# Two transformer layers on one core: slot order of the last down weights, block 3's stores, and the order of squares in layer 1's projection

## The chip, the cores and the metric

The kernel runs on one core of a Trainium2 chip. The time is the device time of one execution in microseconds (us). The engines have queues of their own and run side by side: TensorE (PE) does matmuls, VectorE (DVE) and ScalarE (ACT) work element by element, GpSimd (POOL) does small vector work and issues DMAs, and SyncE (SP) issues DMAs. Each engine works through its own queue in order, so an instruction that waits holds everything behind it on that engine.

## The reference, cut to what matters

```python
def _A_ref(x, wqkv, wo):          # S = 2048 rows, D = 448, 16 heads of 28
    qkv = (x @ wqkv) ...          # split into q, k, v by head
    scores = einsum("bhqd,bhkd->bhqk", q, k) * (Dh ** -0.5)
    o = einsum("bhqk,bhkd->bhqd", softmax(scores), v)
    return o ... @ wo

def _B_ref(x, w_gate, w_up, w_down):        # F = 1792
    return (sigmoid(x @ w_gate) * (x @ w_up)) @ w_down

x = x + _A_ref(layernorm(x), ...)
x = x + _B_ref(layernorm(x), ...)
x = x + _A_ref(layernorm(x), ...)
x = x + _B_ref(layernorm(x), ...)
```

All of it is in float32. The kernel splits each float32 factor into a high and a low float16 part and sums three products for one.

## The kernel before

**Order.** Two layers follow each other. Each is project (layer norm, q, k and v), attend, out_project and gated (the feed-forward). The 2048 rows are 4 blocks of 512, a block is 4 tiles of 128. The order of instructions on every engine is written out by hand: the order of the Python calls is the order of each queue.

**Fast products.** gated, and in layer 1 also the q/k products of blocks 0, 2 and 3 (qk_sums, L884), use a scheme of seven products of half matrices in place of eight. Its operands are sums and differences of quarter matrices. For rows they are made by half_steps into the tiles xwide and xshort; for the q/k weights add_pair (L748) makes them out of raw weights (tile raws) into wsums, five microseconds of DVE work with ACT beside it. There are three pairs of weight tiles (PAIRS_QK); the seventh weight tile is alone and is multiplied in the usual way (L998). Block 1 takes the usual product (qk, L618).

**The end of gated.** The down product of one block is seven products too, with weights dn, one tile of 784 KB for each. The products of block 3 have nothing to run beside, so they come last, in the order TAIL = (0, 1, 3, 2, 5, 4, 6). Product k adds into PSUM bank 3, 1, 3, 2, 3, 1, 3 for k = 0 to 6, except that k = 6 uses banks 0 and 2 here; finish (L1882) lets DVE add a bank to the rows x. Each of the seven takes 42 matmuls. Three dn tiles are held; used_dn (L1766) gives one back and loads the next on POOL's queue (L1758). A list called between puts the preparation of layer 1 between the products: norms, lifts and transposes of block 2's rows (squared, L333 to L358), store and gather (L391, L399), which turn them round through DRAM, and add_pair(2).

**Slots.** SBUF is managed as 19 equal slots (class Slots, "_s" in names) and 12 quarter slots ("_q"). get takes the first of a queue of free slots, put gives a slot back at its end and put_next at its front. A tile in a slot waits for the last user of the tile that was there. So the order of get and put decides which load waits for whom.

**Layer 1's start.** project for layer 1 runs in this order: q/k of block 0 (qk_sums), its values (vals, L1084, evacuated by ACT at L1102), q/k of block 1 (qk), its values, q/k of block 2 and of block 3 (qk_sums), values of blocks 2 and 3. In qk_sums three Pairs use PSUM banks 0 and 1, 2 and 3, and 6 and 7, each a chain and a side. ACT copies each product off the chain (L956) ahead of the next one there. Then high (ACT, L917) and low (DVE, L921) cut a finished tile into its parts and store it. square (ACT, L932) and two maxima (DVE, L936) bound the norms of heads; small matmuls (norms, L899) sum them into a bank, and finish (L1067) reduces it. The work named in points and after is done between products: it prepares the rows of the blocks to come.

Of the kernel before, what the change touches and what calls it, by code (L numbers as in the profile page):

```python
# [13 lines left out]
F16 = mybir.dt.float16  # L14
# [5 lines left out]
P = 128  # L20
S = 2048
D = 448
# [99 lines left out]
def interleaved_layers(ctx: ExitStack, tc: tile.TileContext, x_in, wqkv, wo, w_gate, w_up,  # L122
# [531 lines left out]
    class WeightsQKV:  # L654
# [65 lines left out]

        def read_pairs(self):
            self.raws = [big.get("raws", [P, 2, 1024]) for _ in range(2)]
            for j, tiles in enumerate(PAIRS_QK):
                v = self.pair(j)
                for z, i in enumerate(tiles):
                    c = slice(i * P, (i + 1) * P)
                    nc.gpsimd.dma_start(v[:, 0:3, z],
                                        wqkv[0:384, c].rearrange("(s p) n -> p s n", p=P))
                    nc.gpsimd.dma_start(v[0:64, 3, z], wqkv[384:448, c])
                nc.gpsimd.memset(v[64:P, 3], 0.0)  # L730

        def pair(self, j):
            return self.raws[j // 2][:, j % 2].rearrange("p (s z n) -> p s z n", s=4, z=2)

        def load(self):
            self.v = big.get("wv", [P, 2, 4, D], F16)
            self.more = more = big.get("wmore", [P, 8 * P + D], F16)
            self.alone = more[:, 0:8 * P].rearrange("p (i k n) -> p i k n", i=2, k=4)
            self.v_tail = more[:, 8 * P:]
            c = slice(ALONE * P, (ALONE + 1) * P)  # L740
            for i in range(2):
                nc.sync.dma_start(self.alone[:, i, 0:3], qk_parts[i, :, 0:3, c])
                r = slice(64 * i, 64 * i + 64)
                nc.sync.dma_start(self.alone[r, 0, 3], qk_parts[i, r, 3, c])
                nc.sync.dma_start(self.v_tail[r], v_parts[r, i, 3])
            nc.sync.dma_start(self.v, v_parts)
            self.sums = []

        def add_pair(self, j):
            v, t = self.pair(j), big.get("wsums", [P, N_SUMS, P], F16)  # L750
            self.sums.append(t)
            m = [int(i > ALONE) for i in PAIRS_QK[j]]
            by = up[:, m[0]:m[0] + 1]
            if m[0] != m[1]:
                for z in range(2):
                    nc.vector.tensor_scalar(v[:, :, z], v[:, :, z], up[:, m[z]:m[z] + 1], None,
                                            op0=ALU.mult)
                by = ones[:, 0:1]
            split_sums(t, v, by)
            if j > 0:  # L760
                big.put(self.raws[j // 2])

# [51 lines left out]
    def project(layer, wq, begun):  # L814
# [68 lines left out]

        def qk_sums(b, blk, points, before=None):  # L884

# [97 lines left out]
            for t in range(2):  # L983
                for q in (0, 2):
                    x = blk.quarter(q, t)
                    for k in range(2):
                        if q + k == 3:
                            terms += [(t, wq.alone[:, 0, 3], x[:, i, 1]) for i in range(2)]
                        else:
                            terms += [(t, wq.alone[:, i, q + k], x[:, j, k])  # L990
                                      for i, j in ((0, 0), (0, 1), (1, 0))]
# [11 lines left out]
            pb.first()  # L1003
            at(0)
            pa.apart()
            pa.second()
# [8 lines left out]
            if before:  # L1015
                before()
            pa.c11_c22()
# [8 lines left out]
            pa.c12()  # L1026
            pb.c12()
            alone = bank(5 - b % 2, "alone")
            pc = Pair(2, 6)
# [24 lines left out]
            pc.tiles[1].high()  # L1054
            pc.tiles[1].low(pc.two)
            pa.tiles[1].square()
            pb.tiles[1].square()
            lone.square()
            pc.tiles[0].square()
            pc.tiles[1].square()  # L1060
            at(5)

            def finish(whole=True):
                pop(len(late) - (0 if whole else 1))
                if whole:
                    for k in range(2):
                        nc.vector.tensor_reduce(peaks[:, k, b:b + 1],  # L1067
                                                pn[0:H, k * P:(k + 1) * P], axis=AX.X,
                                                op=ALU.max)
            return finish  # L1070
# [91 lines left out]
        else:  # L1162
# [16 lines left out]
            fin = qk_sums(3, b3, {}, fin)  # L1179
        if layer > 0:  # L1180
            big.put(*wq.sums)
            evac[0] = 0
# [50 lines left out]
        def last_values(begun=None):  # L1233
# [6 lines left out]
            if layer > 0:  # L1240
                big.put(wq.v, wq.more)

# [485 lines left out]
    class WeightsGated:  # L1728
# [36 lines left out]

        def used_dn(self):  # L1766
            (big.put_next if self.pairs else big.put)(self.dn.popleft())
            if self.products:
                self.load_dn(nc.gpsimd)

    def gated(layer, first, wt, wq):
# [243 lines left out]
        for b, p in seq:  # L2015
# [58 lines left out]
            if b == NB - 1 and not last and p == NP - 2:  # L2074
                wq.read_pairs()

# [153 lines left out]
```

## Time and profile before

| | us |
|---|---|
| median of 3 runs | 1909.7 |
| lowest, highest | 1909.0, 1911.4 |
| the profiled execution, in all | 1910.1 |
| its span, first to last instruction | 1908.4 |

The mean TensorE clock granted over the span is 0.996 of full speed. The page's busy strip for PE and its clock strip:

```profile
PE   9999999999999999999898999999999999999999
...
PEclk9999999999999999999899999999999999999999
```

Each digit is the busy share of a fortieth of the span (47.7 us) in tenths; 9 is 90% or more. Digits 20 to 23, 906 to 1097 us, hold the end of layer 0 and layer 1's projection. In a row of a timeline stand the start, the length, the engine, the line of the kernel, the operation, out<-in, the shape and the count of instructions merged; in square brackets the idle time ahead of it and what ended it. A row of the list of waits reads: engine, what it was to do, what it waited for, then the total in us, how often, and the longest. A row of the window table gives the stretch, its length, the busy time of PE, PE's weight loads, DVE, ACT and POOL with counts, PE's clock, and the DMA engines' share and GB/s.

### The profile page before, as it was taken

What the parts mean: (1) busy time and instruction counts of PE and PEld (TensorE: products, weight loads), DVE (VectorE), ACT (ScalarE), POOL (GpSimd) and SP (SyncE); (2) the same over time, 40 slices, a digit from 0 to 9 for tenths busy, and PEclk for the clock granted to TensorE, in tenths of its full rate; (3) what the DMA queues carried; (4) which work ended last, traced back from release to release, by engine and by line L of the source; (5) the groups of instructions that cost most, each with busy time, mean ns of one, the idle gap of its engine ahead of it and who ended that gap; (6) DMA issues with size and microseconds to landing.
All of it is one profiled execution on the core that took longest, in us unless ns stands there. A gap on an engine that the chain in (4) does not pass through costs nothing. (4 is left out here: it accounts for less than half of the span.)

```text
span 1908.4 us, 57171 instructions
## 1 busy us (share of the span) xinstructions
PE 1884.7 (99%) x24531; PEld 1364.3 (71%) x24531; DVE 1478.9 (77%) x2984; ACT 1425.9 (75%) x1885; POOL 250.5 (13%) x482
## 2 busy tenths in 40 slices
PE   9999999999999999999898999999999999999999
PEld 4456655556566899999776566666666668999999
DVE  7758989898977887778776577877787788877664
ACT  6569999999984655555466799999999746555541
POOL 3023102222102012112310000000000021111110
PEclk9999999999999999999899999999999999999999
DMA  7675444343324745656543411221120246566553
GB/s 250 192 217 160 133 122 131 111 124 117 102 87 131 252 177 206 238 206 244 182 151 105 115 47 31 52 51 33 46 52 12 73 148 231 196 228 225 216 207 140
DMA packets 116472, 273.79 MB, mean 143 GB/s; under 512 B 14478, under 2 KB 72590, under 8 KB 116080
## 3 DMA queue, kind: packets, MB, share of 16 engines
q0 software_dynamic: 33120, 163.33, 23.8%
q1 hardware_dynamic: 81936, 105.33, 19.7%
q8 instruction: 194, 3.18, 0.7%
q10 hardware_dynamic: 1152, 1.38, 0.3%
q14 instruction: 70, 0.57, 0.1%
HBM read 210.98 MB, written 50.62 MB: 137 GB/s over the span
## 5 line engine op out<-in xcount | busy, mean ns | idle before, releaser
L1519 ACT ACTIVATE prob_s<-sc 128x1536 f32<-128x1536 f32 (+1 forms) x657 | 888.7, 1477 | 7.5 <-PE sc L1504 6.8
L1555 PE MATMUL acc<-prob_s,val_s 128*32 128x256 f32 (+3 forms) x7700 | 575.0, 384 | 0.1
L1504 PE MATMUL sc<-qp_s 114*32 114x512 f16 x7868 | 558.1, 379 | 0.7 <-DMA qp_s<-g_scr 0.7
L633 PEld LDWEIGHTS <-gu_s 128*128 128x128 f16 x4368 | 426.7, 98 | 46.1 <-PE op L1684 0.7
L1504 PEld LDWEIGHTS <-qp_s 114*32 114x32 f16 x8192 | 279.8, 96 | 198.3 <-issue 84.9
L1555 PEld LDWEIGHTS acc<-prob_s,val_s 128*32 128x32 f32 x7700 | 282.0, 110 | 130.3 <-issue 12.8
L1864 PE MATMUL dnp<-dn_s,hparts_s 128*128 128x224 f16 x2184 | 248.9, 261 | 8.0 <-DMA dn_s<-dn_parts 8.0
L633 PE MATMUL chain<-xwide_s,gu_s 128*128 128x256 f16 x2016 | 247.5, 273 | 0.1
L1864 PEld LDWEIGHTS <-hparts_s 128*128 128x128 f16 x2184 | 211.9, 99 | 14.4 <-DMA dn_s<-dn_parts 8.2
L1535 DVE SCALAR_TENSOR_TENSOR power_q<-power_q,expo_q 128x512 f32<-128x512 f32 x243 | 168.2, 692 | 8.3
L1937 ACT COPY one_q<-chain 128x256 f32<-128x256 f32 x224 | 82.3, 372 | 113.5 <-PE chain L633 113.0
L1953 DVE TENSOR_TENSOR one_q<-side,one_q 128x512 f32<-128x512 f32 x112 | 72.1, 686 | 96.0 <-PE side L633 95.7
L633 PE MATMUL side<-xshort_s,gu_s 128*128 128x256 f16 x1120 | 140.6, 273 | 0.0
L1745 POOL DMA_DIRECT2D gu_s<-gu_parts x104 | 56.5, 543 | 428.0 <-PE side L633 426.5
L1817 ACT CAST hparts_s<-hsums_q 128x256 f16<-128x256 f32 (+1 forms) x152 | 71.5, 485 | 37.0 <-DVE hsums_q L1829 23.4
L1584 DVE STREAM_TRANSPOSE oturned_q<-acc 128x512 f32<-128x512 f32 x32 | 22.9, 717 | 98.2 <-PE acc L1555 98.1
L1555 PE MATMUL acc<-power_q,val_s 128*32 128x256 f32 (+3 forms) x300 | 94.2, 396 | 0.0
L633 PE MATMUL side<-xwide_s,gu_s 128*128 128x256 f16 x672 | 91.6, 273 | 0.0
L618 PE MATMUL qkp<-xhl_s,wqk_s 128*128 128x512 f16 x385 | 86.5, 379 | 0.9 <-ACT wqk_s L235 0.6
L1964 ACT ACTIVATE one_q<-one_q 128x512 f32<-128x512 f32 x56 | 35.3, 630 | 64.2 <-DVE one_q L1953 64.0
L1529 DVE TENSOR_SCALAR expo_q<-aside,base 128x512 f32<-128x512 f32 x81 | 60.6, 748 | 22.5 <-PE aside L1504 22.3
L1821 DVE TENSOR_TENSOR hparts_s<-hsums_q,hparts_s 128x256 f16<-128x256 f32 (+1 forms) x152 | 72.5, 516 | 5.8 <-ACT hparts_s L1817 5.8
(261 smaller groups left out, 2398.7 us busy)
## 6 DMA issues: line engine op xcount, KB each, us to landing
gu_s<-gu_parts POOLq DMA_DIRECT2D x104, 800.0 KB, 5.9
dn_s<-dn_parts POOLq DMA_DIRECT2D x42, 784.0 KB, 7.2
qp_s<-qk_scr SPq DMA_DIRECT2D x96, 224.0 KB
gu_parts<-pack_s POOLq DMA_DIRECT2D x14, 800.0 KB, 3.8
xt_scr<-xs_s SPq DMA_DIRECT2D x48, 224.0 KB
xraw_s<-xt_scr SPq DMA_DIRECT2D x12, 768.0 KB
qk_scr<-qkhl_q SPq DMA_DIRECT2D x35, 256.0 KB
qp_s<-qk_scr SPq DMA_DIRECT2D x64, 112.0 KB
```

Source lines behind the costliest of these rows:

```text
L618: nc.tensor.matmul(pm, w, x, start=(i == 0), stop=(i == len(terms) - 1))
L633: nc.tensor.matmul(pm, a, x, start=(first and i == 0), stop=(i == len(terms) - 1), skip_group_check=True)
L1504: nc.tensor.matmul(ps[32 * j:32 * j + 32, :], hd.k[:, keys], hd.q[:, qb * W:(qb + 1) * W], start=True, stop=True, tile_position=(0, 32 * j))
L1519: nc.scalar.activation(prob[:, 0:n, :], ps[:, 0:n, :], AF.Exp, scale=exp_scale)
L1529: nc.vector.tensor_scalar(y, ps, base2[:, 0:1], -126.0, op0=ALU.mult, op1=ALU.max)
L1535: nc.vector.scalar_tensor_tensor(p, p, c[k], y, op0=ALU.add, op1=ALU.mult)
L1555: nc.tensor.matmul(acc[qb * VC:(qb + 1) * VC, s], v[:, kc % TB, h, :], probs[c * NB + qb][:, s], start=(kc == 0 and a == 0), stop=(kc == N ...
L1817: nc.scalar.copy(to[:, :, 0], a)
L1821: nc.vector.tensor_tensor(to[:, :, 1], a, to[:, :, 0], op=ALU.subtract)
L1864: nc.tensor.matmul(pm, a[:, x, t], w[:, p, y], start=(begin and n == 0 and (j == 0 or alone)), stop=(n == 2), skip_group_check=True)
L1937: nc.scalar.copy(to, pm)
L1953: nc.vector.tensor_tensor(one[m], side[m], one[m], op=ALU.add)
```

## The change

It edits two places. **In gated of layer 0**, only pairs 0 and 1 of the raw q/k weights are read ahead, into one slot; pair 2 is read later, between the second and the third of the last products. Three more dn tiles are loaded ahead of add_pair(0), so that six of the seven are asked for before the last products begin, and a finished dn slot goes to the front of the queue. The tiles wv and wmore are no longer taken here: the lone weights and the last rows of the values' weights (v_tail) go into unused columns of the wsums tiles (now 32 wide), and they and wv are loaded ahead of the last product. **In layer 1's project**, the norms of block 3 move into block 0's q/k products and its lifts, transposes and store into block 0's values, in place of block 2's half steps, which move into block 1's products. In qk_sums the lone tile is cut ahead of the third pair's first tile, the squares of the first two pairs' second tiles are spread between products, and block 2 leaves three squares (lone and third pair) to block 3, which does them one by one (before(False)) and reduces block 2's norms after its second c12.

```diff
-        def read_pairs(self):
-            self.raws = [big.get("raws", [P, 2, 1024]) for _ in range(2)]
+        def read_pairs(self, js):
+            self.raws = big.get("raws", [P, 2, 1024])
...
         def load(self):
-            self.v = big.get("wv", [P, 2, 4, D], F16)
-            self.more = more = big.get("wmore", [P, 8 * P + D], F16)
...
-            nc.sync.dma_start(self.v, v_parts)
-            self.sums = []
+            self.held, self.sums = [], []
         def add_pair(self, j):
-            v, t = self.pair(j), big.get("wsums", [P, N_SUMS, P], F16)
+            v, t = self.pair(j), big.get("wsums", [P, 32, P], F16)
+            self.held.append(t)
+            self.sums.append(t[:, 0:N_SUMS])
...
+        def load_rest(self):
+            self.alone = [t[:, 28:32] for t in self.held[1:]]
+            self.v_tail = self.held[0][:, N_SUMS:29].rearrange("p k n -> p (k n)")[:, 0:D]
+            c = slice(ALONE * P, (ALONE + 1) * P)
+            for i in range(2):
+                nc.sync.dma_start(self.alone[i][:, 0:3], qk_parts[i, :, 0:3, c])
+                r = slice(64 * i, 64 * i + 64)
+                nc.sync.dma_start(self.alone[0][r, 3], qk_parts[i, r, 3, c])
+                nc.sync.dma_start(self.v_tail[r], v_parts[r, i, 3])
+        def load_values(self):
+            self.v = big.get("wv", [P, 2, 4, D], F16)
+            nc.sync.dma_start(self.v, v_parts)
...
-        def qk_sums(b, blk, points, before=None):
+        def qk_sums(b, blk, points, before=None, defer=False):
...
             pb.first()
             at(0)
+            if before:
+                before(False)
...
             if before:
-                before()
+                before(False)
             pa.c11_c22()
...
             pb.c12()
+            if before:
+                before()
             alone = bank(5 - b % 2, "alone")
...
             pc.c11_c22()
+            pa.tiles[1].square()
             pop()
             some(10)
             lone = Tile(alone, ((ALONE, 0), (ALONE, 1)))
             pc.c21()
+            lone.high()
+            lone.low()
             pc.tiles[0].high()
             pc.tiles[0].low(pc.one)
-            lone.high()
-            lone.low()
-            pop()
             pc.c12()
+            pb.tiles[1].square()
+            squares = deque([lone.square, pc.tiles[0].square, pc.tiles[1].square])
+            if not defer:
+                squares.popleft()()
             pc.tiles[1].high()
             pc.tiles[1].low(pc.two)
-            pa.tiles[1].square()
-            pb.tiles[1].square()
-            lone.square()
-            pc.tiles[0].square()
-            pc.tiles[1].square()
+            while squares and not defer:
+                squares.popleft()()
...
             def finish(whole=True):
+                if not whole:
+                    squares.popleft()()
+                    return
...
-            fin = qk_sums(0, blks[0], {0: ready[0:1], 1: ready[1:2], 2: ready[2:3],
-                                       4: ready[3:4]})
-            vals(0, blks[0], {0: both(*h2[0:2]), 1: both(*h2[2:3], s3[0]),
-                              2: both(fin, h2[3]), 3: both(s3[1], h2[4])})
-            fin = qk(1, b1, [both(s3[2], s3[3], s3[6]), both(s3[4], s3[5], s3[7], s3[8]),
-                             both(s3[9], b3.store), both(h2[5], b3.gather), h2[6], h2[7], h2[8]],
-                     None)
+            fin = qk_sums(0, blks[0], {0: ready[0:1] + s3[0:1], 1: ready[1:2], 2: s3[1:2],
+                                       4: ready[2:3], 5: ready[3:4]})
+            vals(0, blks[0], {0: both(s3[2], s3[3], s3[6]), 1: both(fin, s3[4], s3[7]),
+                              2: both(s3[5], s3[8], s3[9], b3.store),
+                              3: both(h2[0], h2[1], b3.gather)})
+            fin = qk(1, b1, h2[2:9], None)
...
-            fin = qk_sums(2, b2, {0: h3[6:7], 1: h3[7:8], 2: h3[8:9], 4: h3[9:10]})
+            fin = qk_sums(2, b2, {0: h3[6:7], 1: h3[7:8], 2: h3[8:9], 4: h3[9:10]}, None, True)
             fin = qk_sums(3, b3, {}, fin)
...
-        def used_dn(self):
-            (big.put_next if self.pairs else big.put)(self.dn.popleft())
+        def used_dn(self, reuse=False):
+            (big.put_next if self.pairs or reuse else big.put)(self.dn.popleft())
...
-                wq.read_pairs()
+                wq.read_pairs((0, 1))
...
             wq.load()
+            for _ in range(3):
+                wt.load_dn(nc.gpsimd)
             wq.add_pair(0)
             wq.add_pair(1)
...
-            between = deque([turns[0:1], turns[1:2], turns[2:5] + turns[6:8],
-                             turns[5:6] + turns[8:] + [third.store],
-                             [third.gather, lambda: wq.add_pair(2)], []])
+            between = deque([turns[0:1], [lambda: wq.read_pairs((2,))] + turns[1:2],
+                             turns[2:5] + turns[6:8], turns[5:6] + turns[8:] + [third.store],
+                             [third.gather, lambda: wq.add_pair(2)],
+                             [wq.load_rest, wq.load_values]])
...
-            wt.used_dn()
+            wt.used_dn(not last)
```

More of the change, by code (lines that the diff above doesn't have):

```diff
@@ L732, in pair @@
         def pair(self, j):
-            return self.raws[j // 2][:, j % 2].rearrange("p (s z n) -> p s z n", s=4, z=2)
+            return self.raws[:, j % 2].rearrange("p (s z n) -> p s z n", s=4, z=2)
         def load(self):
-            self.v = big.get("wv", [P, 2, 4, D], F16)
-            self.more = more = big.get("wmore", [P, 8 * P + D], F16)
[L738 to L745, printed above, removed]
-            nc.sync.dma_start(self.v, v_parts)
-            self.sums = []
+            self.held, self.sums = [], []
         def add_pair(self, j):
-            v, t = self.pair(j), big.get("wsums", [P, N_SUMS, P], F16)
-            self.sums.append(t)
+            v, t = self.pair(j), big.get("wsums", [P, 32, P], F16)
+            self.held.append(t)
+            self.sums.append(t[:, 0:N_SUMS])
             m = [int(i > ALONE) for i in PAIRS_QK[j]]
@@ L759, in add_pair @@
             split_sums(t, v, by)
-            if j > 0:
-                big.put(self.raws[j // 2])
+            self.to_add -= 1
+            if not self.to_add:
+                big.put(self.raws)
+        def load_rest(self):
[10 more added lines that the diff above has]
+            nc.sync.dma_start(self.v, v_parts)
         def load_usual(self):
@@ L987, in qk_sums @@
                         if q + k == 3:
-                            terms += [(t, wq.alone[:, 0, 3], x[:, i, 1]) for i in range(2)]
+                            terms += [(t, wq.alone[0][:, 3], x[:, i, 1]) for i in range(2)]
                         else:
-                            terms += [(t, wq.alone[:, i, q + k], x[:, j, k])
+                            terms += [(t, wq.alone[i][:, q + k], x[:, j, k])
                                       for i, j in ((0, 0), (0, 1), (1, 0))]
@@ L1240, in last_values @@
             if layer > 0:
-                big.put(wq.v, wq.more)
+                big.put(wq.v, wq.held[0])
         return values, heads, last_values
```

17 lines of the change are left out of this document (8 added, 9 removed).

## The prediction, as it was made before the result was known

> **What bounds the kernel now.** I read the page's busy shares first, then TensorE's list of waits, then the timeline and the window table around each wait.
>
> ```profile
> PE 1884.7 (99%) x24531; PEld 1364.3 (71%) x24531; DVE 1478.9 (77%) x2984; ACT 1425.9 (75%) x1885; POOL 250.5 (13%) x482
> ```
> ```profile
> PE dnp L1864 <- DMA dn_s<-dn_parts: 8.0, 1, 8.0
> PE chain L633 <- ACT one_q L956: 3.3, 1, 3.3
> PE chain L633 <- ACT val_s L1102: 1.6, 1, 1.6
> ...
> PE norms L899 <- DVE sq_q L936: 0.9, 4, 0.3
> PE side L633 <- ACT val_s L1102: 0.7, 1, 0.7
> PE side L633 <- DVE one_q L972: 0.7, 2, 0.4
> ```
>
> TensorE (PE) is busy 99% of the span, so an edit pays only if it removes PE's idle time or makes PE run faster. The idle time is a short list, and all six rows lie in one stretch, 923 to 1060 us: the end of layer 0's feed-forward and layer 1's projection, which is what the diff edits. Their sum, 15.2 us, is not the whole prize: a busy matmul can be a slow one.
>
> ```profile
> 945.10:951.00 5.90, 5.83 (x32) 4.76 (x33) 0.00 (x0) 0.72 (x2) 0.00 (x0) 0.50 0.61 244
> 1014.60:1033.00 18.40, 15.73 (x143) 13.59 (x142) 12.24 (x27) 13.86 (x34) 0.00 (x0) 1.00 0.20 58
> 1038.50:1041.00 2.50, 2.47 (x25) 2.15 (x25) 0.28 (x2) 1.00 (x3) 0.00 (x0) 0.77 0.20 58
> 1041.00:1043.00 2.00, 2.00 (x11) 1.45 (x10) 0.00 (x0) 0.00 (x0) 0.00 (x0) 0.50 0.00 0
> ```
>
> In this window table the number ahead of the last two is PE's granted clock. Behind the 8.0 us wait it is 0.50 for 5.9 us: 2.95 us lost. Behind the 3.3 us wait it is 0.77 over 2.5 us and 0.50 over 2.0 us: 0.23 x 2.5 + 0.5 x 2.0 = 1.6 us lost. In the second row PE idles 1.56 and 0.75 us within 4 us and the clock stays 1.00. So I take gaps up to about 2.3 us as free of a clock loss and one of 3.3 us as not.
>
> **The change, part by part.** Times below are those of the profiled execution before.
>
> *A. The last down weights.*
>
> ```profile
> 923.80 13.39 PE L1864 MATMUL dnp<-dn_s,hparts_s 128*128 128x224 f16 x138
> 945.17 19.14 PE L1864 MATMUL dnp<-dn_s,hparts_s 128*128 128x224 f16 x168 [7.97 <-DMA dn_s<-dn_parts]
> 964.14 1.52 PE L633 MATMUL chain<-xwide_s,wsums_s 128*128 128x256 f16 x12
> ...
> 973.70 0.49 PE L998 MATMUL alone<-xwide_s,wmore_s 128*128 128x256 f16 x3
> ```
> ```profile
> 938.71 0.53 POOL L1758 DMA_DIRECT2D dn_s<-dn_parts  x1 [14.42 <-DVE wsums_s L266]
> ```
> ```profile
> 938.20 0.68 DVE L1882 SCALAR_TENSOR_TENSOR x<-dnp,back,x 128x448 f32<-128x448 f32 x1
> ...
> 956.90 0.87 DVE L756 TENSOR_SCALAR raws_s<-raws_s,up 128x512 f32<-128x512 f32 x2
> ...
> 962.13 1.83 DVE L1882 SCALAR_TENSOR_TENSOR x<-dnp,back,x 128x448 f32<-128x448 f32 x3
> ```
>
> PE stops at 937.2 because the fourth product's weights were asked for at 938.71 only: their slot was that of the raw q/k weights, which DVE's split of pair 1 holds until 938.2. With the diff, only one raw slot is taken, wv and the lone tile take none yet, and three loads stand in POOL's queue before add_pair(0). Counting the slot queue by hand gives the fourth product the slot of the last gate weights, free at 923.7, the fifth that of block 1's transposed rows (xs), and the sixth a down slot free at 925. The 8.0 us wait and the 2.95 us of half clock go.
>
> *What is late next.* The fourth product (k=2) adds into the bank of the first (k=0), and DVE reads that bank with the add at 938.20, behind both splits in its queue. So PE restarts at about 938.9: 1.7 us of idle remain. From there 168 matmuls at full clock (138 took 13.39 us, 97 ns each) take 16.2 us, to 955.1.
>
> The moved read_pairs((2,)) puts four DMAs and a memset into POOL's queue between the two norm_two of block 2:
>
> ```profile
> 911.73 0.78 POOL L727 DMA_DIRECT2D raws_s<-in_A_wqkv_dram  x1
> ...
> 913.83 0.54 POOL L729 DMA_DIRECT2D raws_s<-in_A_wqkv_dram  x1
> 914.36 0.33 POOL L730 MEMSET raws_s<- 64x256 f32 x1
> ...
> 941.88 0.22 POOL L346 TENSOR_SCALAR off<-off 128x2 f32<-128x2 f32 x1
> ...
> 942.80 0.18 POOL L333 TENSOR_SCALAR rs<-mv 128x2 f32<-128x2 f32 x1
> ...
> 944.15 0.23 POOL L346 TENSOR_SCALAR off<-off 128x2 f32<-128x2 f32 x1
> ```
>
> They cost 914.69 - 911.73 = 3.0 us. The first norm_two ends at 942.1, the DMAs at 945.1, the second (1.6 us) at 946.7. ACT's two lifts and DVE's two transposes behind them (0.7 us each, overlapping) end at 948.7, the fifth product's add at 949.3, add_pair(2) (956.90 to 962.13, 5.2 us) at 954.5, and the three adds (1.83 us) at 956.4. Bank 0 is read by the third, and layer 1's first product writes bank 0. PE is there at 955.1 and starts at 956.5: **1.4 us of new idle**. The start moves from 964.14 to 956.5: **-7.6 us** (8.0 + 2.95 - 1.7 - 1.4 = 7.8 by terms; I take the timeline). For the new idle, bounds are 0, if the raws' issues overlap DVE's work, and 4, if the raws land late and the clock halves too; 1.4 is what the rows give.
>
> The fifth load waits for the xs store, and all of POOL's queue behind it: the sixth and seventh loads and norm_two, of which nothing else is due before 940.5.
>
> ```profile
> 926.96 3.55 SPq L391 DMA_DIRECT2D xt_scr<-xs_s  x4
> 933.75 0.38 SPq L399 DMA_DIRECT2D xraw_s<-xt_scr  x1
> ...
> 934.84 0.46 SPq L742 DMA_DIRECT2D wmore_s<-qk_parts  x1
> ...
> 937.68 0.60 SPq L745 DMA_DIRECT2D wmore_s<-v_parts  x1
> ...
> 954.06 3.61 SPq L391 DMA_DIRECT2D xt_scr<-xs_s  x4
> 960.71 0.38 SPq L399 DMA_DIRECT2D xraw_s<-xt_scr  x1
> ```
> ```profile
> DMA to landing us min/median/max: 4.2/7.1/12.5
> ```
>
> The gather, which waits for that store, is issued at 933.75, so the fifth load goes out then and lands 4.2 to 12.5 us later, 938.0 to 946.3; PE needs it at 942.9. By the median (940.9) it is in time, at the maximum PE waits 3.4 us. load_rest (six DMAs) and the wv load now stand on SP's queue behind block 2's gather: the store moves from 954.06 to 948.8 and the gather, 6.65 us after it as before (960.71), to 955.5; its two DMAs take 0.9 us and load_rest's six 3.4 (934.84 to 938.28), so load_rest is out by 959.8 and, with the best landing of a far larger load (4.2), there by 964; the lone tile's first use is 9.6 us after layer 1's start (973.70 against 964.14 before), 966.1. I cost it at nothing; its cover is 2 us thick.
>
> *B. Block 3's rows stored in block 0's values.*
>
> ```profile
> 1012.47 0.71 ACT L453 CAST xwide_s<-xraw_s 128x256 f16<-128x256 f32 x2 [3.29 <-DMA xraw_s<-xt_scr]
> ```
> ```profile
> 1010.65 0.28 DVE L880 TENSOR_REDUCE peaks<-knorm 16x1 f32<-16x128 f32 x1 [1.74 <-PE knorm L841]
> 1012.48 0.76 DVE L445 TENSOR_TENSOR t_q<-xraw_s 128x256 f32<-128x256 f32 x2 [1.54 <-DMA xraw_s<-xt_scr]
> ```
>
> Block 3's gather lands at 1012.47 and holds ACT and DVE; the val_s evacuations queued behind it make PE wait 1.56 + 0.75 = 2.3 us. Stored some 10 us sooner, the gather is no longer last: DVE then waits for PE's norms (the reduce at 1010.65) and starts 1.54 us sooner. ACT's chain moves by the same: **-1.5 us**, and 0.8 stay. Block 3's lifts and transposes enter block 0's values, block 2's half steps leave it for the usual product. There PE has 16.8 us of its own and DVE 15.75, ACT 14.2 before; the swap takes out more than it puts in:
>
> ```profile
> 989.20:1006.00 16.80, 16.80 (x81) 7.70 (x80) 15.75 (x42) 14.21 (x28) 4.86 (x9) 1.00 0.42 105
> ```
>
> Without that cover it would be up to 3 us. finish one tile sooner in block 0's values may cost 0 to 0.5 us, as DVE's last maxima end there about when PE comes: I take 0.3.
>
> *C. Squares spread and deferred.*
>
> ```profile
> 1035.00 0.63 ACT L917 ACTIVATE qkhl_q<-two_q 128x512 f16<-128x512 f32 x1 [1.26 <-DVE two_q L979]
> 1035.54 2.69 ACT L932 ACTIVATE sq_q<-qkhl_q 128x512 bf16<-128x512 f16 x5
> 1038.14 0.62 ACT L956 COPY one_q<-chain 128x256 f32<-128x256 f32 x2
> ```
> ```profile
> 1038.53 1.50 PE L633 MATMUL chain<-xwide_s,wsums_s 128*128 128x256 f16 x12 [3.28 <-ACT one_q L956]
> ```
>
> Five squares stand between block 2's last high and block 3's first copy. With the diff two of them fill earlier waits of ACT (1.26 us on DVE here) and three go to block 3. ACT's copy follows the high, at 1035.4, and is done 0.3 later; PE resumes at about 1035.8. **-2.7 us, and the 1.6 us of half clock go.** Against it: block 3 now pops six norms and reduces them after the second c12, and its lone tile's bank is the one reduced; DVE does the two adds first, so PE waits about 0.5 us. Net **-3.8**. By hand count the three held tiles leave the 12 quarter slots just enough, and no slot is taken whose last user is still at work.
>
> [...]
>
> *D. Block 3's end.* The four waits of norms on DVE's squares (0.9 us) shrink as two squares, not five, remain after the last high: **-0.7**. The waits on L972 (0.7) stay: the step ahead of them is unchanged.
>
> *Sum.* 7.6 + 1.5 + 3.8 + 0.7 - 0.3 = 13.3 us. The profiled execution took 1910.1 (span 1908.4 and 1.7 around it): 1896.8. The median of the runs is 0.4 below it: **1896.4**.
>
> **Rivals.**
>
> 1. *Fuller gain.* The residues (1.7, 1.4, 0.8, 0.6, 0.5, 0.3) do not appear because POOL, ACT and DVE also run ahead. 13.3 + 5.3 = 18.6: 1891.1. Against it: 1.7 and 0.8 follow from DVE's own rows. Chance 0.10.
>
> 2. *A transfer takes the place of the one removed.* The fifth weights (at the 12.5 us maximum, 3.4 us late) or the lone tile (by some 2 us more than its cover) stop PE, and the clock halves for one more stretch (1.6). 13.3 - 5 = 8.3: 1901.4. For it: in the trace the fourth load took 6.5 us against 4.2 at best while SP's transfers ran. Against it: wv and the lone tile are out of its way now. [...] Chance 0.16.
>
> 3. *The tail is kept apart in name only.* The lone tile and the values' tail now lie inside the wsums tiles. If readers wait for a whole tile, pair 1's first product waits until load_rest lands: to about 964 from 957.2, 6.8 us, and 2.5 us of clock. 13.3 - 9.3 = 4.0, or rather less: 1906 to 1908, **no change that can be told**. Against it: the memset at 914.36 into a raw tile follows a DMA into other rows of it, issued at 913.83, without a wait. Chance 0.06.
>
> 4. *Slower.* POOL's queue at the fifth load. If the xs store is held up by the two loads now running beside it, loads five to seven go out late one behind the other, and PE, at half clock after each gap, loses half of the 12 us of tail as well. It decides when the fifth landing passes 942.9 by 11 us (954): 11 + 6 eats the 13.3 and 4 more; 1914 or above. That needs 20 us from the store's end, against at most 12.5 for any such load. Chance 0.04.
>
> **How the numbers follow.** Forecast 0.64 (11 to 16 us off), fuller 0.10, transfer 0.16, in name only 0.06, slower 0.04. 0.2% is 3.8 us, about what a measurement of this kernel can tell from no change: faster 0.90, same 0.06, slower 0.04. The range, 1891.5 to 1903, holds the forecast and nearly all of the first two rivals; it takes the new idle of A from its bound 0 to 4 and the fifth weights from in time to 3.4 us late.
>
> **What would show it.** A: dn_s gone from PE's waits, POOL's three loads issued at 924 to 935, a first gap of about 1.7 us released by DVE's add, a second of about 1.4 us at layer 1's start, no row of half clock near 945. B: no cast waiting for xraw in block 1's values, val_s waits of about 0.8 in all. C: no gap above 1 us between blocks 2 and 3, clock 1.00 there, a new wait of about 0.5 of the lone tile on peaks. D: norms' waits under 0.3. I am wrong if a DMA still ends a wait of PE in this stretch, or if a residue passes 2.3 us and halves the clock.

## The result, and the profile after

The changed kernel takes a median of **1901.6 us** over six runs (1899.9 to 1903.5), the kernel before 1910.6 over six runs beside it. The ratio is **0.995, interval 0.9937 to 0.9964**: about half a per cent faster, 9.0 us between the medians and 9.6 by the ratio, where 13.3 were forecast. The profiled execution took 1900.5, with a span of 1898.8. First the page's row of busy time and its clock strip:

```profile
PE 1880.8 (99%) x24531; PEld 1385.4 (73%) x24531; DVE 1478.7 (78%) x2984; ACT 1425.2 (75%) x1885; POOL 249.2 (13%) x482
...
PEclk9999999999999999999999999999999999999999
```

The strip of before had one 8, in the edited stretch. It is gone, and yet the busy share still reads 99%: a share over the whole span can't show a change of half a per cent. The list of TensorE's waits in the changed kernel can (total, times, longest):

```profile
PE alone L1004 <- DMA wsums_s<-qk_parts: 2.1, 2, 1.7
PE dnp L1875 <- DVE x L1893: 1.7, 1, 1.7
PE chain L633 <- DVE x L1893: 1.6, 1, 1.6
...
PE side L633 <- DVE one_q L978: 1.0, 2, 0.5
...
PE alone L1004 <- DVE peaks L1080: 0.9, 1, 0.9
...
PE side L633 <- ACT val_s L1114: 0.7, 1, 0.7
...
PE chain L633 <- ACT one_q L962: 0.4, 1, 0.4
```

The 8.0 us on dn_s, the 3.3 on one_q, the 1.6 on val_s and the 0.9 of norms are gone. Two waits on DVE's add into x were forecast (1.7 and 1.4) and came (1.7 and 1.6). The first row was not in the forecast's sum: the lone tile's weights arrive too late. A DMA that still ends a wait of PE in this stretch is what the prediction had named as the sign that it is wrong. The same on TensorE's timeline:

```profile
925.33 13.39 PE L1875 MATMUL dnp<-dn_s,hparts_s 128*128 128x224 f16 x138
940.47 16.26 PE L1875 MATMUL dnp<-dn_s,hparts_s 128*128 128x224 f16 x168 [1.74 <-DVE x L1893]
958.33 1.47 PE L633 MATMUL chain<-xwide_s,wsums_s 128*128 128x256 f16 x12 [1.61 <-DVE x L1893]
...
969.32 0.39 PE L1004 MATMUL alone<-xwide_s,wsums_s 128*128 128x256 f16 x2 [1.66 <-DMA wsums_s<-qk_parts]
970.15 0.28 PE L1004 MATMUL alone<-xwide_s,wsums_s 128*128 128x256 f16 x1 [0.43 <-DMA wsums_s<-qk_parts]
...
1013.12 0.81 PE L633 MATMUL side<-xwide_s,wsums_s 128*128 128x256 f16 x6 [0.75 <-ACT val_s L1114]
...
1030.25 1.47 PE L633 MATMUL chain<-xwide_s,wsums_s 128*128 128x256 f16 x12 [0.44 <-ACT one_q L962]
1039.15 0.50 PE L1004 MATMUL alone<-xwide_s,wsums_s 128*128 128x256 f16 x3 [0.92 <-DVE peaks L1080]
```

And the windows around three of the places where the clock might halve; PE's clock stands ahead of the last two numbers, and it is 1.00 in all:

```profile
940.50:946.40 5.90, 5.90 (x62) 5.90 (x62) 5.68 (x13) 1.41 (x2) 3.81 (x8) 1.00 0.99 375
...
967.60:971.00 3.40, 1.30 (x11) 0.89 (x11) 1.58 (x4) 1.00 (x2) 0.55 (x2) 1.00 0.99 186
...
1029.80:1034.60 4.80, 4.36 (x41) 3.90 (x40) 1.73 (x5) 3.73 (x10) 0.00 (x0) 1.00 0.54 150
```

Where the time went is read from landmarks on that timeline: the start of the last down products, of layer 1's first product, of block 0's values, of block 2's product, of block 3's, of the values of blocks 2 and 3, and of the first score. The stages between them, in us, for both kernels and for the experiments below (no median stands where a kernel has one run only):

| | start | down | qk 0 | to qk 2 | qk 2 | qk 3 | to score | profiled run | median |
|---|---|---|---|---|---|---|---|---|---|
| before | 923.8 | 40.34 | 16.41 | 34.07 | 18.50 | 20.77 | 17.98 | 1910.1 | 1910.6 |
| changed | 925.3 | 33.00 | 18.36 | 34.12 | 16.87 | 17.64 | 16.57 | 1900.5 | 1901.6 |
| e1 lone weights early | 926.7 | 33.22 | 15.92 | 34.12 | 16.87 | 17.64 | 16.14 | 1899.2 | 1899.2 |
| e2 usual weights late | 926.6 | 33.00 | 15.92 | 34.53 | 16.87 | 17.64 | 16.23 | 1899.3 | |
| e3 raws first | 924.8 | 31.71 | 16.38 | 34.12 | 16.87 | 17.64 | 16.10 | 1896.2 | |
| e4 = e1 + e3 | 924.8 | 32.85 | 15.92 | 34.12 | 16.87 | 17.63 | 16.27 | 1897.1 | 1897.4 |
| e5 = e2 + e3 | 925.1 | 31.42 | 15.92 | 34.67 | 16.87 | 17.63 | 16.13 | 1896.5 | 1896.0 |
| e6 layer 0's end only | 925.3 | 33.00 | 18.31 | 34.06 | 18.44 | 22.02 | 17.66 | 1907.4 | 1907.4 |
| e7 layer 1's order only | 924.7 | 39.64 | 15.97 | 34.12 | 16.88 | 17.63 | 16.55 | 1903.5 | 1904.3 |
| e8 no deferral | 925.1 | 32.99 | 20.40 | 34.12 | 16.88 | 17.89 | 16.11 | 1902.6 | |
| e9 changed again | 924.7 | 32.99 | 18.55 | 34.12 | 16.87 | 17.63 | 16.20 | 1899.6 | |
| e10 slots only | 925.3 | 36.96 | 16.40 | 34.06 | 20.23 | 21.85 | 17.94 | 1911.0 | |
| e11 adds later | 925.0 | 33.12 | 19.25 | 34.52 | 16.87 | 17.63 | 16.16 | 1901.2 | 1901.2 |

A stage that nothing disturbs repeats to 0.05 us from kernel to kernel, so differences of half a microsecond can be read here that the times themselves, whose runs spread over 0.7 to 7 us, can't tell. From before to changed: 7.34 gained, 1.95 lost, 0.05 lost, 1.63, 3.13 and 1.41 gained: 11.5. Of that, 1.5 us are missing already at the first landmark, and 0.4 go behind the first score: 9.6, the difference of the two profiled executions. The 1.5 us don't come from the edited stretch. Layer 0's first down product, some 235 us ahead of the first edited instruction, starts at 674.90 before and at 676.43 after; in e7, whose edits all lie behind the first landmark, it starts at 675.80. The first landmark lies between 924.7 and 926.7 in the twelve other profiled executions. So 923.8 is likely the lowest draw of a spread that arises early in the kernel; with one profile of before this is not shown.

### The profile page after: what moved, and what is told of

The parts are those of the page before. It is cut to its first block, busy times and chain, and to the rows that moved or that the text cites. A ratio compares the mean times of both kernels' runs of the same rounds, so it can differ in the third digit from the quotient of the medians.

```text
span 1898.8 us, 57166 instructions
## 1 busy us (share of the span) xinstructions
PE 1880.8 (99%) x24531; PEld 1385.4 (73%) x24531; DVE 1478.7 (78%) x2984; ACT 1425.2 (75%) x1885; POOL 249.2 (13%) x482
## 5 line engine op out<-in xcount | busy, mean ns | idle before, releaser
L1515 PEld LDWEIGHTS <-qp_s 114*32 114x32 f16 x8192 | 293.1, 96 | 186.7 <-issue 72.4
L1566 PEld LDWEIGHTS acc<-prob_s,val_s 128*32 128x32 f32 x7700 | 295.4, 110 | 122.6 <-issue 12.5
```

Source lines behind the costliest of these rows:

```text
L1515: nc.tensor.matmul(ps[32 * j:32 * j + 32, :], hd.k[:, keys], hd.q[:, qb * W:(qb + 1) * W], start=True, stop=True, tile_position=(0, 32 * j))
L1566: nc.tensor.matmul(acc[qb * VC:(qb + 1) * VC, s], v[:, kc % TB, h, :], probs[c * NB + qb][:, s], start=(kc == 0 and a == 0), stop=(kc == N ...
```

## The experiments

**The lone tile's weights: place in the queue, or other transfers?** In the changed kernel SP issues them behind the store and the gather of block 2, and POOL issues the usual product's weights, 896 KB each, just before. SP's issues, then POOL's:

```profile
950.76 2.99 SPq L391 DMA_DIRECT2D xt_scr<-xs_s  x4
958.66 0.38 SPq L399 DMA_DIRECT2D xraw_s<-xt_scr  x1
...
959.70 0.80 SPq L760 DMA_DIRECT2D wsums_s<-qk_parts  x1
...
964.36 0.60 SPq L763 DMA_DIRECT2D wsums_s<-v_parts  x1
```
```profile
958.09 1.16 POOL L772 DMA_DIRECT2D wqk_s<-qk_parts  x2
```

The first 96 KB, issued at 959.70, let PE go on at 969.32. Experiment e1 moves them in the queue and leaves the rest:

```diff
-            self.alone = [t[:, 28:32] for t in self.held[1:]]
+            self.alone = [self.held[1][:, 28:32], self.held[0][:, 29:32]]
...
             wq.add_pair(1)
+            wq.load_rest()
...
-                             [wq.load_rest, wq.load_values]])
+                             [wq.load_values]])
```

> The lone tile's weights are issued right after the second pair's add, ahead of the third block's store and gather on SP, and the second half of them goes into the first pair's slot, so that it does not need the third. Theory 'place in SP's queue' (the weights wait in the queue behind store and gather, issued at 959.7 and not landed before 969): the two waits of L1004 on wsums_s<-qk_parts inside the first layer-1 product, 1.66 and 0.43 us, go, and that stage takes 16.3 to 16.6 us instead of 18.36; whole time 1899 to 1900.5. Rival 'these loads land late wherever they stand, because transfers of other queues share the DMA engines': the waits stay at 1 us or more. Second rival 'something else is late next': the waits go and the stage still takes over 17.5 us.

The waits of L1004 went, qk 0 took 15.92, the median was 1899.2 (ratio 0.9937, 0.9922 to 0.9952). That fits the queue, but also any theory by which an early load lands early. Experiment e2 leaves them where they are and moves the other queue's transfers behind them:

```diff
-            wq.load_usual()
...
-            fin = qk_sums(0, blks[0], {0: ready[0:1] + s3[0:1], 1: ready[1:2], 2: s3[1:2],
+            fin = qk_sums(0, blks[0], {0: ready[0:1] + s3[0:1], 1: ready[1:2], 2: [wq.load_usual] + s3[1:2],
```

> The two loads of the usual query and key weights on POOL's queue (issued at 958.1 and 959 in the changed kernel, one us ahead of the lone tile's weights) are moved into the third point of the first layer-1 product, behind the lone tile's weights. Theory 'place in SP's queue': the weights are issued at 959.7 as before and land about as late; L1004's waits stay at 1.5 to 2.1 us. Rival 'the other queue's transfers delay the landing': from issue to landing falls from 9.5 to 5 or 6 us, and the waits of L1004 go or fall below 0.7 us.

My own theory, that the place in SP's queue is the cause, falls. SP issued the first lone weights at 960.64, 1.1 us after layer 1's start at 959.55 (1.4 us after it in the changed kernel), and yet PE waits for nothing; TensorE's timeline in e2:

```profile
968.07 0.82 PE L633 MATMUL chain<-xwide_s,wsums_s 128*128 128x256 f16 x6
968.72 0.49 PE L1004 MATMUL alone<-xwide_s,wsums_s 128*128 128x256 f16 x3
```

What differs is in the DMA view from 959 to 964: packets, MB and the time that they took as a share of all 16 engines. The changed kernel, then e2:

```profile
q0 software_dynamic: 182, 1.19, 66.7%
q1 hardware_dynamic: 166, 0.34, 21.3%
```
```profile
q1 hardware_dynamic: 522, 0.93, 58.5%
```

With POOL's loads (software_dynamic) in the window, SP's queue (hardware_dynamic) moved 0.34 MB; without them 0.93. The changed kernel's two shares, 66.7% and 21.3%, come to 88.0% of the 16 engines' time. There PE went on 9.6 us after the issue of the first 96 KB; in e2 it uses them 8.1 us after their issue without a wait. So an earlier place in SP's queue suffices as a cure (e1), and so does taking the other queue's 1.8 MB out of the way (e2): in these runs the lone weights, at their place, were late only beside those transfers.

**The gap at layer 1's start.** Experiment e3 reads the third pair's raw weights one step earlier on POOL:

```diff
-            between = deque([turns[0:1], [lambda: wq.read_pairs((2,))] + turns[1:2],
+            between = deque([[lambda: wq.read_pairs((2,))] + turns[0:1], turns[1:2],
```

> The third pair's raw weights are read one step earlier on POOL's queue, before the first norm of the third block's squares instead of between the two. Theory 'the chain POOL, ACT, transposes, add of the third pair, DVE's adds makes the 1.6 us gap at layer 1's start': the second norm starts about 0.84 us earlier on POOL, and the gap in front of the first L633 chain matmul falls from 1.61 to 0.8 us or less. Rival 'the gap is DVE's own work and not POOL's': it stays at 1.4 to 1.7 us, because DVE reaches its adds no earlier. The L1004 waits stay.

```profile
956.49 1.47 PE L633 MATMUL chain<-xwide_s,wsums_s 128*128 128x256 f16 x12 [0.32 <-DVE x L1893]
...
966.33 0.28 PE L1004 MATMUL alone<-xwide_s,wsums_s 128*128 128x256 f16 x1 [0.29 <-DMA wsums_s<-qk_parts]
```

The gap fell from 1.61 to 0.32, as the chain from POOL to DVE's adds says. The lone tile's wait nearly went with it, which was not expected: SP's gather went out at 954.47 and the lone weights at 956.16, 0.3 us ahead of layer 1's start and not 1.4 behind it. The landing was no faster: the second 96 KB, for which PE waits here, were issued at 957.97, beside POOL's loads (956.84 on), and let PE go on 8.4 us later; in the changed kernel they were issued at 962.17 and it took 8.0. One edit took both waits, the second by an earlier issue. Experiment e4 is e1 and e3 together.

> The lone tile's weights early and the third pair's read early together. If both waits go and nothing takes their place: 2.1 + 1.0 to 1.6 us less than the changed kernel, 1897.8 to 1898.8, ratio to the kernel before 0.993 to 0.994. If an earlier start of the product only makes the next weights later (the values' weights or the normed rows): 1899.5 or more, ratio 0.9945 or more.

1897.4 (ratio 0.9928, 0.9914 to 0.9941), but the gap came back to 1.45. DVE's timeline says why; e3 first, then e4:

```profile
949.11 0.49 DVE L747 TENSOR_SCALAR raws_s<-raws_s,up 128x512 f32<-128x512 f32 x1 [0.27 <-DMA raws_s<-in_A_wqkv_dram]
949.76 0.49 DVE L747 TENSOR_SCALAR raws_s<-raws_s,up 128x512 f32<-128x512 f32 x1 [0.16 <-DMA raws_s<-in_A_wqkv_dram]
```
```profile
949.67 0.49 DVE L747 TENSOR_SCALAR raws_s<-raws_s,up 128x512 f32<-128x512 f32 x1 [0.84 <-DMA raws_s<-in_A_wqkv_dram]
950.88 0.49 DVE L747 TENSOR_SCALAR raws_s<-raws_s,up 128x512 f32<-128x512 f32 x1 [0.71 <-DMA raws_s<-in_A_wqkv_dram]
```

The only difference between the two is the earlier load of the lone weights, issued from 936.27 on. The third pair's raws, issued from 939.69 on as in e3, land 1.1 us later beside it. Experiment e5 takes the other cure, e2, with e3.

> The third pair's read one step earlier on POOL, and the usual query and key weights later on POOL, with the lone tile's weights left where the change puts them. By the runs so far (the earlier read takes the gap at layer 1's start from 1.6 to 0.3 us, the later load takes the lone tile's 2.1 us) the two are independent: gap 0.3 us, no wait of L1004 in the first layer-1 product, 3.3 us less than the changed kernel, 1896 to 1898.5 us, ratio to the kernel before 0.9920 to 0.9930. Rival: what is late next takes one of them back (the usual weights themselves at the second block's product, or the value weights), a new wait of over 1 us in the first three layer-1 stages, ratio 0.994 or more.

**1896.0 us, ratio 0.9914 (0.990 to 0.9928): faster than both kernels** (the changed kernel's interval begins at 0.9937). Both waits are gone (0.2 us or less); 0.5 us come back in the stage up to block 2, with no single wait above 0.3.

**The two halves by themselves.** Experiment e6 takes only the diff's part for the end of layer 0 (L718 to L757, the lone tile's terms, used_dn, the order of between); experiment e7 only the part inside project (order of squares, lone tile and norms, the stages of the half steps).

> Only the end of layer 0 is changed (down weights' slots, third pair's raws on their own, the lone tile's weights in the sums' tiles); layer 1's order of squares, norms and steps is that of the kernel before. If the parts add up: the stretch from the last product of layer 0 to the first of layer 1 takes 33.0 us as in the changed kernel (40.3 before), the lone tile's wait of about 2 us is there, and layer 1's later stages keep their old times (18.5, 20.8 and 18.0 us for the third product, the fourth and the rest up to the first score): 1904 to 1906 us, ratio 0.9965 to 0.9975. If the parts hang together (the half clock behind the fourth product or the normed rows' wait comes from the late start): the later stages shorten too and it comes below 1903.

> Only layer 1's order is changed (third block stored during the first block's values, squares spread and the third block's left to the fourth, lone tile first); the end of layer 0 and the slots are those of the kernel before. If the parts add up: the third product, the fourth and the rest up to the first score take 16.9, 17.6 and 16.6 us as in the changed kernel (18.5, 20.8, 18.0 before), the end of layer 0 keeps its 40.3 us with 8 us of down weights' wait: 1904 to 1906 us, ratio 0.9965 to 0.9975. If they hang together: one of the three stages keeps at least 1 us more than in the changed kernel.

e6: 1907.4 (ratio 0.9977, 0.9963 to 0.9991); e7: 1904.3 (0.9959, 0.9944 to 0.9974). The stages add up: e6 has the changed kernel's 33.00 and 18.31, e7 its 16.88, 17.63 and 16.55. Three of e6's seven runs lie in the expected band, at 1905.3 to 1905.4; its median does not. In the profiled run, which is the median, the gap ahead of block 3 stayed 3.28 us and cost more clock than before (22.02 against 20.77). So part A, the larger by forecast, is the smaller by itself: it brings the lone tile's wait with it, and it leaves that gap and its clock loss in place.

**Deferral or spreading?** In e8 block 2 squares its last tiles at its own end.

```diff
-            fin = qk_sums(2, b2, {...}, None, True)
+            fin = qk_sums(2, b2, {...}, None, False)
...
-                    squares.popleft()()
+                    (squares.popleft() if squares else pop)()
```

> As the changed kernel, but the third block squares its own last tiles at its own end; its norms and peaks are still taken inside the fourth block's product. Tells the deferral from the spreading. If the deferral carries the gain between the third and fourth products: the wait for the first copy out of the chain (0.44 us) grows to 1.4 us or more, and the fourth product's stage gives back 1 to 1.5 us of the 3.1. If spreading alone is enough: the stage stays within 0.4 us of 17.64 us. If deferral costs more than it brings (squares of the third block sit ahead of the fourth's copies): the stage is shorter than 17.6.

```profile
1033.01 1.47 PE L633 MATMUL chain<-xwide_s,wsums_s 128*128 128x256 f16 x12 [1.36 <-ACT one_q L962]
...
1041.19 0.50 PE L1004 MATMUL alone<-xwide_s,wsums_s 128*128 128x256 f16 x3 [0.47 <-DVE peaks L1080]
```
```profile
1031.57 1.13 ACT L938 ACTIVATE sq_q<-qkhl_q 128x512 bf16<-128x512 f16 x2
1032.61 0.74 ACT L962 COPY one_q<-chain 128x256 f32<-128x256 f32 x2
```

The first wait grew to 1.36 as expected, but the stage lost only 0.25 (17.89 against 17.64), in large part because the wait on peaks halved from 0.92. ACT's rows say why the gap stays well under the 3.28 of before: two squares stand ahead of block 3's first copy, where five stood. So 2.88 of part C's 3.13 us stay without the deferral. Spreading, with the lone tile cut earlier and block 2's norms taken in block 3, carries them; these three were not tried apart. The run is slower for another reason: its lone wait, by the same code as in the changed kernel, was 2.14 + 0.33, and its windows read

```profile
967.30:970.40 3.10, 0.63 (x4) 0.24 (x4) 1.61 (x4) 1.00 (x2) 0.59 (x2) 0.98 0.91 143
970.40:973.70 3.30, 3.30 (x17) 2.26 (x16) 0.00 (x0) 0.45 (x2) 0.00 (x0) 0.50 0.92 305
```

PE's clock is 0.50 for 3.3 us, 1.65 us lost; qk 0 took 20.40.

**The changed kernel again.**

> The changed kernel once more, unaltered, for one profile: its runs so far lie between 1899.9 and 1903.5 us with mean clocks of 1.0 in the two fastest and 0.999 in the other four. Theory 'the wait on the lone tile's weights stands on the edge of the clock': where the wait of L1004 is 2.3 us or more in all, the clock halves for about 3 us behind it and the first layer-1 product takes about 20.4 us, as in the run without the deferral; where it is 2.1 us or less, the clock stays at 1.0 and it takes 18.4 us. Rival 'the spread of its runs comes from before the stretch': the product takes 18.4 us with the clock at 1.0 and a time above 1901 goes with a late start of the last down products (925 us and more). The third to sixth stages take 16.9, 17.6 and 16.1 to 16.6 us whatever the time.

The wait was 1.87 + 0.41, the clock stayed at 1.00, qk 0 took 18.55, the run 1899.6. The later stages repeat. That slower runs of the changed kernel (up to 1903.5) carry such a stretch of half clock behind the lone tile is likely by e8, but none of them was profiled: argued, not shown.

**The slots without the early issue.** Experiment e10 is the kernel before with used_dn's reuse alone.

```diff
-        def used_dn(self):
-            (big.put_next if self.pairs else big.put)(self.dn.popleft())
+        def used_dn(self, reuse=False):
+            (big.put_next if self.pairs or reuse else big.put)(self.dn.popleft())
...
-            wt.used_dn()
+            wt.used_dn(not last)
```

> The kernel before, with one edit: the last down weights go into the slots that the down products give back, ahead of the others, instead of into those of the sums' raw weights. Nothing is issued earlier, the raws stay together. Theory 'what counts is that the fourth load no longer waits for the sums': the fourth down product's wait of 8.0 us falls to 5 or 6 us (the load is issued when the first of the three last products is through, and takes as long to land as before), still long enough to halve the clock; the stretch takes 37 to 39 us instead of 40.3. Rival 'the early issue carries all': the wait stays at 7.5 us or more. Third: the wait goes altogether (below 2 us), and the slots alone make up part A; the stretch takes 33 to 34 us.

```profile
943.96 18.41 PE L1864 MATMUL dnp<-dn_s,hparts_s 128*128 128x224 f16 x168 [5.32 <-DMA dn_s<-dn_parts]
```
```profile
1017.00:1020.60 3.60, 3.60 (x21) 2.56 (x20) 0.91 (x3) 1.78 (x6) 0.00 (x0) 0.57 0.00 0
```

Slot order by itself gives 3.4 of part A's 7.3; the rest comes with its other edits, the early issue first of all, which were not tried one by one. The run as a whole gained nothing (1911.0): it began 1.5 us later, the stage of block 3 lost 1.1 more than before, and the two waits on val_s, 1.65 and 0.75 us, this time cost clock (second row, 0.57), which 1.56 and 0.75 had not done before (1.00).

**A further step.** Experiment e11 goes on from e5 and moves DVE's two sums behind the adds that PE waits for.

```diff
-            wq.add_pair(1)
...
-            between = deque([[lambda: wq.read_pairs((2,))] + turns[0:1], turns[1:2],
+            between = deque([[lambda: wq.add_pair(1), lambda: wq.read_pairs((2,))] + turns[0:1], turns[1:2],
...
-                             [third.gather, lambda: wq.add_pair(2)],
-                             [wq.load_rest, wq.load_values]])
+                             [third.gather],
+                             []])
...
+            wq.add_pair(2)
+            wq.load_rest()
+            wq.load_values()
```

> The kernel with the earlier read and the later usual weights, and on DVE the second pair's add behind the first of the last residual adds, the third pair's behind the last of them (the lone tile's weights are loaded behind that). If DVE's order is what leaves the gap of 1.74 us in front of the fourth down product and the 0.3 us ahead of layer 1: both go, layer 1 starts 29.5 us after the last products' start instead of 31.4, and the time is 1894 to 1895. If the third pair's sums, 5.5 us of DVE, now come too late for the pair of products that uses them (8 us after layer 1's start), or the lone tile's weights do: a wait of 1 us or more in the first layer-1 product, and the time stays at 1896 or above.

```profile
944.40 13.90 PE L1874 MATMUL dnp<-dn_s,hparts_s 128*128 128x224 f16 x126 [1.97 <-DVE x L1892]
...
962.88 1.47 PE L633 MATMUL chain<-xwide_s,wsums_s 128*128 128x256 f16 x12 [2.56 <-ACT one_q L962]
```
```profile
941.71 0.47 DVE L266 SCALAR_TENSOR_TENSOR wsums_s<-raws_s,up,wsums_s 64x256 f16<-64x256 f32 x1
942.21 0.63 DVE L329 BATCH_NORM_STATS2 st<-x 128x6 f32<-128x448 f32 x1
...
943.70 0.65 DVE L1892 SCALAR_TENSOR_TENSOR x<-dnp,back,x 128x448 f32<-128x448 f32 x1
```
```profile
960.57 1.39 ACT L263 ACTIVATE wsums_s<-sums_q,ones 128x512 f16<-128x512 f32 x2 [0.75 <-DVE sums_q L254]
...
962.48 0.62 ACT L962 COPY one_q<-chain 128x256 f32<-128x256 f32 x2
```

It did not help: 1901.2 (ratio 0.995, 0.9935 to 0.9965). The gap ahead of the fourth down product went and came back one product later, 1.97 us: by DVE's rows the second pair's sums, up to 942.2, and 1.5 us of block 2's row statistics behind them still stand ahead of the add at 943.70. And the third pair's sums hold not only DVE: ACT's share of them stands ahead of its copy off the chain, so PE waits 2.56 us for ACT. Neither theory had named ACT.

## Why the forecast was right in direction and short in size

- **A, forecast 7.6, measured 7.34.** Right in its mechanism and residues: the wait on dn_s went, PE stopped 1.74 us for DVE's add (forecast 1.7) and 1.61 at layer 1's start (1.4), the fifth load was in time. Experiment e3 shows that POOL's moved read made the second, and e10 how much is slot order.
- **load_rest "at nothing; its cover is 2 us thick": the step that failed.** It cost 2.4 us (18.36 against 15.92 where the wait is gone). Set against layer 1's start I had the gather 1.0 us before it; it went out 0.3 after it. I had the six issues take 3.4 us; they took 5.3 (959.70 to 964.96). And I gave the landing 4.2 us, the best of all loads. I looked at SP's queue and left out that load_usual, which the diff does not touch, now starts on POOL at the same moment. e2, where it starts later, has no wait. The forecast had a rival for it, a transfer that takes the place, at 1901.4 with a chance of 0.16. Its lone tile's half came, without its half clock in the profiled run (1.00). That the median, 1901.6, lies beside that 1901.4 is luck: the rival took off 5 us for a late transfer and its half clock, and this wait cost 2.4.
- **B, forecast 1.5, measured 1.63**; 0.75 us of the wait on val_s stays, as said (0.8). The 0.3 us for finish one tile sooner did not come (0.05).
- **C, forecast 3.8, measured 3.13**, and 0.44 more in block 0's product that the forecast did not have (16.41 against 15.97 in e7). The gap fell by 2.84 (forecast 2.7), the half clock went (1.00), but the lone tile waits 0.92 on peaks, not 0.5. The waits on one_q that were to stay at 0.7 came at 1.0. e8 corrects the reason: what it leaves in place, the squares in ACT's earlier waits above all, does it; putting three off to block 3 is worth 0.25.
- **D, forecast 0.7, measured 1.41.** I counted the printed waits of norms, 0.9 us. Start to start the same rows say more. TensorE's timeline before, then after, from the first norms to the next product:

```profile
1058.05 0.22 PE L899 MATMUL norms<-sq_q,ind 128*128 128x64 bf16 x2
1058.43 0.23 PE L899 MATMUL norms<-sq_q,ind 128*128 128x64 bf16 x2 [0.16 <-DVE sq_q L936]
1058.93 0.29 PE L899 MATMUL norms<-sq_q,ind 128*128 128x64 bf16 x4 [0.26 <-DVE sq_q L936]
1059.45 0.23 PE L899 MATMUL norms<-sq_q,ind 128*128 128x64 bf16 x2 [0.23 <-DVE sq_q L936]
1059.97 0.23 PE L899 MATMUL norms<-sq_q,ind 128*128 128x64 bf16 x2 [0.29 <-DVE sq_q L936]
1060.04 1.87 PE L1084 MATMUL vp<-wv_s,xshort_s 128*128 128x448 f16 x9
```
```profile
1049.48 0.66 PE L905 MATMUL norms<-sq_q,ind 128*128 128x64 bf16 x14
1049.97 1.87 PE L1096 MATMUL vp<-wv_s,xshort_s 128*128 128x448 f16 x9
```

1.99 us became 0.49: the stall is 1.5. Part of it is in the printed lengths and not in the printed waits: the five rows before have 1.20 us of length for 12 matmuls, the one row after 0.66 for 14.

In sum: the terms of the forecast came to 13.5 instead of 13.3, which is luck, as errors cancel, plus the 0.44 in block 0's product. The lone tile took 2.4, which gives the 11.5 of the table; 1.5 and 0.4 are the two executions' own difference outside the edited stretch, and the median lies 1.1 above the profiled run. With the one step mended, e1 takes 1899.2 and e2 1899.3, some 2.8 us above the forecast; their profiled executions reach the first landmark 2.9 and 2.8 us later than that of before. e5's 1896.0 lies within half a microsecond of the forecast by luck: it also removes the gap at layer 1's start, which the forecast had counted as staying.

## What to carry to other kernels

When a step pulls work ahead, look at what every other queue issues in the same few microseconds, the unedited lines too; here a transfer was late by what ran beside it, and not only by its place in its own queue (PE waited 2.09 us for the lone weights beside POOL's loads, and not at all in e2, where those came later). Give a load that has a thin cover the worst landing of a load of its size under traffic, not the best of the page (in the changed kernel PE went on 8.0 and 9.6 us after the issues, where the forecast had 4.2). Cost a stall by the distance from start to start (1.5 us at the norms, where the waits print 0.9), and compare stages between landmarks: undisturbed ones repeat here to 0.05 us where whole runs spread over 0.7 to 7.

## What the runs showed of the hardware

The forecast took gaps of PE up to about 2.3 us as free of clock loss. The runs show no such bound: 1.66 + 0.43 (changed) and 1.87 + 0.41 us (e9) left the clock at 1.00, 2.14 + 0.33 (e8) and 1.65 + 0.75 (e10) cost clock, and within e11 a single gap of 1.97 us cost clock (first row: 0.57 over 4 us) while one of 2.56 did not (second row the gap, third the time behind it):

```profile
944.40:948.40 4.00, 4.00 (x25) 3.34 (x26) 2.18 (x6) 1.04 (x2) 3.47 (x9) 0.57 0.93 331
...
960.30:962.90 2.60, 0.04 (x2) 0.02 (x1) 2.60 (x7) 2.33 (x5) 0.00 (x0) 1.00 1.15 302
962.90:966.00 3.10, 3.10 (x29) 2.78 (x29) 2.99 (x8) 2.29 (x6) 0.52 (x2) 1.00 1.05 271
```

So from 1.97 to 2.56 us the length of a gap does not tell the two kinds apart in these runs; why one cost clock and another did not is not shown. Here a stall of 1.97 to 2.56 us cost its own length in one place and 1.5 to 1.7 us more in another (1.65 in e8, 0.43 x 3.6 in e10, 0.43 x 4.0 in e11), so it has to be priced with both ends.
